# Softmax sums of a head pair: one transpose and a broadcast through DRAM in place of six transposes, and GpSimd in place of VectorE for the scaling

## The chip, the cores and the metric

The kernel runs on one core of a Trainium2 chip. A core has five engines that run their own instruction streams in order: TensorE (PE, with a queue of weight loads PEld beside it), VectorE (DVE), ScalarE (ACT), GpSimd (POOL) and SyncE (SP, which here only issues DMAs). The metric is the device time in microseconds (us) of one execution, lower is better.

## The reference

```python
# q, k, v: (2, 8, 768, 64); centroids: (8, 16, 64)
q_assign = np.argmax(np.einsum('bhsd,hcd->bhsc', q_n, c_n), axis=-1)
k_assign = np.argmax(np.einsum('bhsd,hcd->bhsc', k_n, c_n), axis=-1)
mask = q_assign[:, :, :, None] == k_assign[:, :, None, :]
scores = np.where(mask, scale * np.matmul(q, k.transpose(0, 1, 3, 2)), -1000000000.0)
scores = scores - np.max(scores, axis=-1, keepdims=True)
attn = np.exp(scores)
attn = attn / (np.sum(attn, axis=-1, keepdims=True) + 1e-09)
x = np.matmul(attn, v)            # heads side by side: (1536, 512)
h = np.maximum(np.maximum(x @ w1, x @ w2), x @ w3)     # w: 512 x 768
x = h @ w_out                                          # 768 x 512
h = x @ w_in                                           # 512 x 2048
return np.maximum(0.01 * h, h) @ w_out2                # 2048 x 512
```

The change is about the division of `attn` by its row sums.

## The kernel before

The kernel first does attention (to about 255 us of the span) and then two feed-forward layers. Attention goes over 8 pairs of heads (4 pairs for each of the 2 batches). The two heads of a pair lie on the two halves of the 128 partitions. A pair has 6 units: unit `n` is pair `n // 6`, head `j` (0 or 1) and block `g` of 256 queries (0 to 2), in the order j=0: g=0,1,2, then j=1: g=0,1,2. I call these units r0 to r5.

For one unit the stages are: scores on PE (`scores`, L569, into one of two score banks in PSUM), row maxima on DVE (`maxima`, L575), exponentials on ACT that also sum the rows (`exps`, L581), transposes of the exponentials on PE (`transposes`, L618), a split of each into a rounded part `eh` and a rest `el` (on ACT, DVE and POOL by turns, L635, L639, L647, L650), and the product with `v` on PE (`values`, L663). The product lands in the first half of a PSUM bank `o`, as head dim by query, that is transposed. `move` (L682) and `keep` (L688) add it into `acc`, the SBUF buffer that holds the attention output with head dims on partitions and queries in the free dimension.

The sums are made the other way round: `rs` has one query per partition (128 partitions by 12 numbers a pair: 3 blocks, 2 half blocks of 128 queries, 2 heads). To scale `acc`, they must stand along the free dimension and on all 64 partitions of their head. Before the change this is done once per block, when the second head's unit (r3, r4, r5) is through:

- `widen` (L605, POOL) copies the four inverse sums of a partition into `rb`, 64 times each: 128 x 256;
- `spread` (L672, PE) transposes the two 128 x 128 halves of `rb` into the second half of the unit's `o` bank, called `r`;
- `scale` (L692, DVE) multiplies 128 x 256 of `acc` by `r`.

There is no automatic scheduler. The table `ORDER` has one row per unit of a pair and says in which order the program issues stages: `SP/1` is `spread` for the unit one before the present one, `K1/2` is `keep` for the unit two before, `S0/-2` the scores of half block 0 of the unit two ahead, `D0+1` a stage of the next pair. `BEGIN` and `END` list what happens before the first and after the last unit. The names used below: `RB` widen, `SP` spread, `K2` scale, `RA` and `RC` sums and their inverse, `D0` and `D1` the operands of the next pair, `LD` loads of q, k, v.

`D0` and `D1` (`operands`, L504) are 16 copies from SBUF to SBUF, issued by SP: they put the split q and k of a pair in the layout that the scores want. `D0` is ten copies of 64 x 768 floats (five for head 0, five for head 1), `D1` is per head one such copy (`kl`) and two of 16 x 768 (`oo`, the mask's one-hot rows). SP runs its DMAs in program order: one whose source is not ready holds up all that stand behind it. A DMA also waits until the eighth DMA before it has landed, since eight semaphores are used in turn.

The next pair's first scores, in row 4 of `ORDER` (`S0/-2` with unit r4), are four matmuls: two read `q1`, `k1` (from `D0`, head 0), two read `q2`, `k2` (from `D0` and `D1`, head 0).

Of the kernel before, what the change touches and what calls it, by code (L numbers as in the profile page):

```python
# [8 lines left out]
F32 = mybir.dt.float32  # L9
# [3 lines left out]
ALU = mybir.AluOpType  # L13
# [4 lines left out]
P = 128  # L18
B, H, S, D = 2, 8, 768, 64
C = 16  # L20
NP = H // 2
NPAIR = B * NP
NQ = S // P
G = 256
NG = S // G
# [10 lines left out]
BIG = 2.0**100  # L36
ORDER = (
# [13 lines left out]
)  # L51

# [6 lines left out]

END = (  # L60
    "E10:47 B4:46 K2:45 RB:46 E12:47 h h V0:46 L0:47 L4:46 E14:47 V2:46 V4:46 SP:46 B2:47 E24:47 Y:46 L2:47 "
    "K1:46 RC:47 h h h h L4:47 K2:46 RB:47 V0:47 V2:47 V4:47 SP:47 h Y:47 K1:47 K2:47"
)

ONCE = {
# [22 lines left out]
def clustered_attention_mlps(  # L88
# [16 lines left out]
    nc = tc.nc  # L105
# [212 lines left out]
    with ExitStack() as att:  # L318
        def pool(stack, name, bufs, space=bass.MemoryType.SB, side="left"):
            return stack.enter_context(  # L320
                tc.tile_pool(name=name, bufs=bufs, space=space, side=side)
            )
# [2 lines left out]
        vp = pool(att, "vp", 2, side="right")  # L325
        etp = pool(att, "etp", 2, side="right")
        sm = pool(att, "sm", 2, side="right")
        ps_t = pool(att, "ps_t", 3, PSUM, "right")
        ps_o = pool(att, "ps_o", 1, PSUM, "right")
        until_transposes = att.enter_context(ExitStack())  # L330
# [8 lines left out]
        idf = const.tile([P, P], F32, name="idf")  # L339
# [9 lines left out]
        st = {}  # L349

        def load_pair(p, what="qkv", queue=nc.sync):
            s = st.setdefault(p, {})
            for x in what:
                if x == "v":
                    s["rv"] = raws.tile([P, NQ, 2, D], F32, tag="rv", name=f"rv{p}")
                    src = v[p].rearrange("p (t h d) -> p t h d", t=NQ, h=2)
                else:
                    s["r" + x] = raws.tile([P, S], F32, tag="r" + x, name=f"r{x}{p}")
                    src = (qT if x == "q" else kT)[p]
                queue.dma_start(out=s["r" + x], in_=src)  # L360

        def engine(op, p):
            return ENGINE.get(f"{op}@{p}", ENGINE[op])
# [16 lines left out]
        def round_q(p):  # L380
            s = st[p]
            s["qh"] = hl.tile([P, S], F32R, tag="qh", name=f"qh{p}")
            rounded(engine("QH", p), s["qh"], s["rq"], SCALE)

        def round_k(p):
            s = st[p]
            s["kh"] = hl.tile([P, S], F32R, tag="kh", name=f"kh{p}")
            rounded(engine("KH", p), s["kh"], s["rk"])

        def rest_q(p):  # L390
            s = st[p]
            s["ql"] = hl.tile([P, S], F32R, tag="ql", name=f"ql{p}")
            rest("D", s["ql"], s["rq"], s["qh"], SCALE)

        def rest_k(p):
            s = st[p]
            s["kl"] = hl.tile([P, S], F32R, tag="kl", name=f"kl{p}")
            rest(engine("KL", p), s["kl"], s["rk"], s["kh"])
# [151 lines left out]
        un = {}  # L550

        def unit(n):
            p, r = divmod(n, 2 * NG)
            j, g = divmod(r, NG)
            return p, j, g
# [44 lines left out]

        def widen(n):
            p, j, g = unit(n)
            rb = sm.tile([P, 2, 2, D], F32, tag="rb", name=f"rb{n}", bufs=3)
            rs = st[p]["rs"][:, g].rearrange("p i (j o) -> p i j o", o=1)
            nc.gpsimd.tensor_scalar(  # L605
                rb, rs.to_broadcast([P, 2, 2, D]), 1.0, 1.0, op0=ALU.mult, op1=ALU.mult
            )
            un[n]["rb"] = rb
# [17 lines left out]
        def way(n, k):  # L626
            return WAYS[n % (2 * NG)][k // 2]
# [38 lines left out]
                    )  # L666


        def spread(n):
            u = un[n]  # L670
            for i in range(2):
                nc.tensor.transpose(  # L672
                    u["r"][:, i * P : (i + 1) * P],
                    u["rb"][:, i].rearrange("p j d -> p (j d)"), idf,
                )
# [13 lines left out]

        def scale(n):  # L690
            a = place(n)
            nc.vector.tensor_tensor(a, a, un[n]["r"], op=ALU.mult)  # L692

        def place(n):
            p, j, g = unit(n)
            c = ((p // NP) * NG + g) * G
            return acc[c // TB][:, p % NP, c % TB : c % TB + G]
# [23 lines left out]
        def do(op, at):  # L721

            o, d = op[:-1], op[-1]
            d = int(d) if d.isdigit() else 0
            if op == "LD":
                load_pair(at)
            elif op == "QH":
                round_q(at)
            elif op == "KH":
                round_k(at)  # L730
            elif op == "QL":
                rest_q(at)
            elif op == "KL":
                rest_k(at)
            elif op == "VH":
                split_v(at, 0)
            elif op == "VL":
                split_v(at, 1)
            elif o == "G":
                sims(at, d, spare(at, op, 2))  # L740
            elif op[0] == "N":
                j = int(op[1])
                if op[2] == "a":
                    near_max(at, j, spare(at, f"G{j}", 2))
                else:
                    near_eq(at, j)
            elif op == "W":
                weigh(at, nc.gpsimd if engine("W", at) == "P" else nc.vector)
            elif op == "FA":
                first_max(at)  # L750
            elif op == "FB":
                first_eq(at)
            elif o == "O":
                onehot_T(at, d, spare(at, op, 1))
            elif op == "SP":
                spread(at)
            elif o == "P":
                penalties(at, d, spare(at, f"O{d}", 1))
            elif o == "D":
                operands(at, 3 * d)  # L760
            elif o == "S":
                scores(at, d)
            elif o in ("SA", "SB"):
                scores(at, d, ("AB".index(o[1]),))
            elif o == "M":
                maxima(at, d)
            elif o == "X":
                exps(at, d)
            elif op == "RA":
                guard(at)  # L770
            elif op == "RC":
                inverse(at)
            elif op == "RB":
                if unit(at)[1] == 1:
                    widen(at)
            elif o == "T":
                transposes(at, d)
            elif o == "E1":
                out_of_psum(at, d, "copy" if way(at, d) == "P" else "hi")
            elif o == "E2":  # L780
                if way(at, d) == "A":
                    out_of_psum(at, d, "copy")
            elif o == "B":
                if way(at, d) == "P":
                    his(at, d)
            elif o == "L":
                rests(at, d)
            elif o == "V":
                values(at, d)
            elif op == "Y":  # L790
                move(at)
            elif op == "K1":
                keep(at)
            elif op == "K2":
                scale(at)
            else:
                raise ValueError(op)

        pieces, scraps = {}, {}
        if True:  # L800
# [104 lines left out]
            for op in BEGIN.split():  # L905
                if "@" in op or ":" in op:
                    op, at = op.replace("@", ":").split(":")
# [3 lines left out]
            for n in range(NU):  # L911
                c, r = divmod(n, 2 * NG)
                items = ORDER[r].split()
                for i in range(len(items) + 1):
# [7 lines left out]
                    if "/" in items[i]:  # L922
                        op, lag = items[i].split("/")
                        at = n - int(lag)
                        if 0 <= at < NU and f"{op}:{at}" not in begun:
                            do(op, at)
                    else:
                        op, ahead = items[i].split("+")
                        at = c + int(ahead)
# [7 lines left out]
            for op in END.split():  # L937
                if op == "h":
                    start(op)
                else:  # L940
                    op, at = op.split(":")
# [71 lines left out]
```

## Time and profile before

| what | value |
|---|---|
| time, median of 3 runs | 707.63 us (707.37 to 708.17) |
| time of the profiled execution | 707.71 us |
| its span (first to last instruction) | 705.9 us |
| PE busy | 699.4 us (99%) |
| DVE, ACT, POOL busy | 527.0 us (75%), 379.6 us (54%), 285.3 us (40%) |
| DMA queue of SP | 88.13 MB, 41.7% of 16 DMA engines |

The busy time of an engine is the union of its instructions. The shares are means over attention and feed-forward, which use the engines differently. A pair of heads takes 29.0 us of the attention stage.

### The profile page before, as it was taken

The page shows a single profiled execution, that of the slowest core. Times are in us where ns is not written, and L with a number is a line of the kernel's source. Part 1 is how long each engine was busy: PE and PEld are TensorE (multiplying, and loading weights), DVE is VectorE, ACT ScalarE, POOL GpSimd, SP SyncE. Part 2 cuts the span into 40 slices and gives each one's busy share as a digit, 9 for nine tenths or more (in the row PEclk, how much of TensorE's full clock was granted, in tenths as well). Part 3 has the DMA queues.
Part 4 walks back from the last instruction along what each step waited for, and adds up shares of the span by engine and source line. Part 5 has one row for each costly group of instructions (what it writes and reads, how often), then busy time and mean ns, then how long its engine had stood idle before and what let it go on. Part 6 is the DMA issues. An engine that isn't in the chain of part 4 may idle for free.

```text
span 705.9 us, 10794 instructions
## 1 busy us (share of the span) xinstructions
PE 699.4 (99%) x3876; PEld 601.4 (85%) x3878; DVE 527.0 (75%) x1008; ACT 379.6 (54%) x725; POOL 285.3 (40%) x263
## 2 busy tenths in 40 slices
PE   9999999999999999999999999999999999999997
PEld 6899999999999888888888888888888888888886
DVE  7888998988998788888884599788439846983222
ACT  6888989988999845322321234455434333431220
POOL 3778888888896611101110101333312233221220
PEclk9999999999999999999999999999999999999999
DMA  3887465384460017645553145245405522600112
GB/s 115 217 255 185 98 202 149 83 236 104 125 160 3 1 41 242 208 165 155 176 165 101 52 156 180 90 130 203 144 16 193 179 91 70 197 32 0 46 45 90
DMA packets 29189, 90.00 MB, mean 127 GB/s; under 512 B 4336, under 2 KB 4336, under 8 KB 29136
## 3 DMA queue, kind: packets, MB, share of 16 engines
q1 hardware_dynamic: 28704, 88.13, 41.7%
q10 hardware_dynamic: 432, 1.18, 0.6%
q8 instruction: 31, 0.51, 0.3%
q14 instruction: 22, 0.18, 0.1%
HBM read 68.16 MB, written 3.15 MB: 101 GB/s over the span
## 4 chain that ended last, share of the span: by engine, by line
PE 97%; ACT 2%; DVE 0%; issue 0%; ACTq 0%
PE h L247 13%; PE h L245 13%; PE h L246 13%; PE o L663 9%; PE s L569 9%; PE t L618 9%; PE y L247 8%; PE y L246 8%; PE y L245 8%; PE s L421 2%; PE warm L815 1%; PE o L672 1%; ACT ee L581 1%; PE scrap L421 1%; PE s L479 1%
## 5 line engine op out<-in xcount | busy, mean ns | idle before, releaser
L279 POOL TENSOR_TENSOR hl<-a,hh 128x512 fp32r<-128x512 f32 x66 | 91.8, 1390 | 344.3 <-ACT hh L278 344.3
L245 PE MATMUL h<-xh,wh 128*128 128x512 f32 x408 | 159.1, 390 | 0.0
L246 PE MATMUL h<-xl,wh 128*128 128x512 f32 x408 | 158.9, 390 | 0.1
L247 PE MATMUL h<-xh,wl 128*128 128x512 f32 x408 | 158.8, 389 | 0.0
L278 ACT CAST hh<-a 128x512 fp32r<-128x512 f32 x66 | 41.1, 622 | 124.9 <-DVE a L272 73.8
L245 PE MATMUL y<-hh,wh 128*128 128x512 f32 x264 | 102.7, 389 | 0.0
L246 PE MATMUL y<-hl,wh 128*128 128x512 f32 x264 | 102.7, 389 | 0.0
L247 PE MATMUL y<-hh,wl 128*128 128x512 f32 x264 | 102.7, 389 | 0.0
L575 DVE TENSOR_REDUCE mx<-s 128x1 f32<-128x768 f32 x96 | 91.2, 951 | 15.0 <-PE s L421 10.8
L650 POOL TENSOR_TENSOR el<-et,eh 128x512 fp32r<-128x512 f32 x72 | 99.2, 1386 | 3.0 <-ACT et L635 0.2
L246 PEld LDWEIGHTS h<-xl,wh 128*128 128x128 f32 x408 | 76.6, 188 | 16.7 <-DVE xl L236 0.8
L569 PE MATMUL s<-k,q 128*128 128x512 f32 (+3 forms) x384 | 89.1, 354 | 1.1 <-ACT oo L496 0.8
L247 PEld LDWEIGHTS h<-xh,wl 128*128 128x128 f32 x408 | 76.6, 188 | 15.8
L245 PEld LDWEIGHTS h<-xh,wh 128*128 128x128 f32 x408 | 76.6, 188 | 15.7
L270 ACT COPY a<-h 128x512 f32<-128x512 f32 x66 | 38.6, 585 | 93.3 <-PE h L247 91.7
L581 ACT ACTIVATE ee<-s,mx 128x768 f32<-128x768 f32 x96 | 86.9, 906 | 3.0 <-DVE mx L575 2.1
L274 DVE SCALAR_TENSOR_TENSOR a<-a,h 128x512 f32<-128x512 f32 x48 | 32.9, 684 | 61.8 <-ACT a L270 61.6
L618 PE MATMUL t<-idf,ee 128*128 128x128 f32 x576 | 78.3, 274 | 0.4 <-DVE el L647 0.4
L305 DVE TENSOR_TENSOR acc<-y,acc 128x512 f32<-128x512 f32 x72 | 48.6, 686 | 40.2 <-PE y L247 40.2
L663 PE MATMUL o<-eh,vs 128*128 128x256 f32 x288 | 73.3, 288 | 0.0
L663 PE MATMUL o<-el,vs 128*128 128x256 f32 x288 | 71.8, 282 | 0.0
L618 PEld LDWEIGHTS t<-idf,ee 128*128 128x128 f32 x576 | 65.4, 142 | 2.7 <-DVE el L647 0.6
(103 smaller groups left out, 1153.2 us busy)
## 6 DMA issues: line engine op xcount, KB each, us to landing
raw<-in_w SPq DMA_DIRECT2D x56, 512.0 KB, 3.9
low<-in_w SPq DMA_DIRECT2D x56, 511.5 KB, 3.6
q<-qh SPq DMA_DIRECT2D x28, 192.0 KB, 3.3
k<-kh SPq DMA_DIRECT2D x28, 192.0 KB, 3.7
out_T<-acc SPq DMA_DIRECT2D x12, 256.0 KB, 2.0
rq<-in_qT SPq DMA_DIRECT2D x7, 384.0 KB, 3.9
rk<-in_kT SPq DMA_DIRECT2D x7, 384.0 KB, 5.8
rv<-in_v SPq DMA_DIRECT2D x7, 384.0 KB, 3.6
```

The costliest lines, as they stand in the source:

```text
L245: nc.tensor.matmul(ps, ah, bh, start=(k == 0), stop=False)
L246: nc.tensor.matmul(ps, ah, bl, start=False, stop=False)
L247: nc.tensor.matmul(ps, al, bh, start=False, stop=(k == n - 1))
L278: nc.scalar.copy(hh[:, f, :], a)
L279: nc.gpsimd.tensor_tensor(hlo[:, f, :], a, hh[:, f, :].bitcast(F32), op=ALU.subtract)
L305: nc.vector.tensor_tensor(a, ps, a, op=ALU.add)
L569: nc.tensor.matmul(ps[:, lo:hi], a[:, c0 : c0 + P], b[:, lo:hi], start=start, stop=not start)
L575: nc.vector.tensor_reduce(mx, un[n]["s", i], axis=AX.X, op=ALU.max, negate=True)
L581: nc.scalar.activation(e, u.pop(("s", i)), AF.Exp, bias=u.pop(("m", i)), scale=1.0, accum_out=u["sum"][:, i, 0:1],)
L618: nc.tensor.transpose(ps[:, kk, i * P : (i + 1) * P], u["e"][i][:, (k + kk) * P : (k + kk + 1) * P], idf,)
L650: nc.gpsimd.tensor_tensor(lo, et, hi.bitcast(F32), op=ALU.subtract)
L663: nc.tensor.matmul(u["o"], vs[:, t, :], u[e][:, t, :], start=(t == 0 and e == "eh"), stop=(t == NQ - 1 and e == "el"),)
```

## The change

For the first seven pairs the sums of the whole pair are handled once, after its last unit r5. `spread` makes one PE transpose of `rs` (128 x 12) into 12 x 128. `K2` then copies that on ACT from PSUM to an SBUF tile `rt` and has SP write it to a DRAM tile `rd` (6 KB). A new stage `RD` (`widely`) reads it back with two DMAs, each onto 64 partitions: `rr` then holds, on every partition, the 6 x 128 inverse sums of the partition's head. Three new stages `K3` (`scale_late`) multiply the three 128 x 256 blocks of `acc` by it on POOL, one to two units later. `widen`, the old `spread` and the old `scale` stay for the eighth pair alone.

In `ORDER`, `RD/3` becomes the first item of row 2 (unit r5 of the pair before). `K3/4` in row 3 scales the block of r5, `K3/8` in row 5 that of r3, and `K3/8` in row 0 of the next pair that of r4. Each `K3` stands right behind an `RB`. `END` gets one `K3:40` as its last item. The code:

```diff
+        dram = pool(att, "dram", 2, bass.MemoryType.DRAM)
...
-            rb = sm.tile([P, 2, 2, D], F32, tag="rb", name=f"rb{n}", bufs=3)
+            rb = sm.tile([P, 2, 2, D], F32, tag="rb", name=f"rb{n}", bufs=1)
...
+        def last(n):
+            return n // (2 * NG) == NPAIR - 1
+
         def spread(n):
             u = un[n]
+            if not last(n):
+                if n % (2 * NG) == 2 * NG - 1:
+                    rs = st[n // (2 * NG)]["rs"].rearrange("p g i j -> p (g i j)")
+                    nc.tensor.transpose(u["r"][0 : 4 * NG, 0:P], rs, idf)
+                return
...
         def scale(n):
             a = place(n)
-            nc.vector.tensor_tensor(a, a, un[n]["r"], op=ALU.mult)
+            if last(n):
+                nc.vector.tensor_tensor(a, a, un[n]["r"], op=ALU.mult)
+            elif n % (2 * NG) == 2 * NG - 1:
+                s = st[n // (2 * NG)]
+                rt = sm.tile([4 * NG, P], F32, tag="rt", name=f"rt{n}", bufs=1)
+                nc.scalar.copy(rt, un[n]["r"][0 : 4 * NG, 0:P])
+                s["rd"] = dram.tile([4 * NG, P], F32, tag="rd", name=f"rd{n}")
+                nc.sync.dma_start(out=s["rd"], in_=rt)
+
+        def widely(n):
+            s = st[n // (2 * NG)]
+            s["rr"] = sm.tile([P, 2 * NG, P], F32, tag="rr", name=f"rr{n}", bufs=1)
+            for j in range(2):
+                rd = s["rd"].rearrange("(x j) q -> j x q", j=2)[j]
+                nc.sync.dma_start(
+                    out=s["rr"][j * D : (j + 1) * D], in_=rd.partition_broadcast(D)
+                )
+
+        def scale_late(n):
+            p, j, g = unit(n)
+            a = place(n)
+            rr = st[p]["rr"][:, 2 * g : 2 * g + 2, :].rearrange("p i q -> p (i q)")
+            nc.gpsimd.tensor_tensor(a, a, rr, op=ALU.mult)
...
-                if unit(at)[1] == 1:
+                if unit(at)[1] == 1 and last(at):
                     widen(at)
```

The order on three engines is shown for one pair (its last unit is 29, and the operands named `_6_` are those of the pair whose first scores come next; the names are the program's with a running number).

On SP, at the operands of that pair, the kernel before had:

```order
L504 DMA q1_6_0_2804<-qh6_2529 64x768
L504 DMA q2_6_0_2805<-qh6_2529 64x768
L504 DMA k1_6_0_2806<-kh6_2660 64x768 x2
L504 DMA q1_6_0_2804<-ql6_2737 64x768
L504 DMA q1_6_1_2813<-qh6_2529 64x768
L504 DMA q2_6_1_2814<-qh6_2529 64x768
L504 DMA k1_6_1_2815<-kh6_2660 64x768 x2
L504 DMA q1_6_1_2813<-ql6_2737 64x768
L504 DMA k2_6_0_2807<-kl6_2789 64x768
L504 DMA q2_6_0_2805<-oo6_2696 16x768
L504 DMA k2_6_0_2807<-oo6_2696 16x768
```

The same place on SP after the change (the next row is the third of `D1`, `k2_6_0` from `oo6`):

```order
L710 DMA rd29_2745<-rt29_2743 12x128
L506 DMA q1_6_0_2780<-qh6_2511 64x768
L506 DMA q2_6_0_2781<-qh6_2511 64x768
L506 DMA k1_6_0_2782<-kh6_2638 64x768 x2
L506 DMA q1_6_0_2780<-ql6_2711 64x768
L506 DMA q1_6_1_2789<-qh6_2511 64x768
L506 DMA q2_6_1_2790<-qh6_2511 64x768
L506 DMA k1_6_1_2791<-kh6_2638 64x768 x2
L506 DMA q1_6_1_2789<-ql6_2711 64x768
L717 DMA rr29_2799<-rd29_2745 64x6x128 x2
L506 DMA k2_6_0_2783<-kl6_2765 64x768
L506 DMA q2_6_0_2781<-oo6_2672 16x768
```

The write of the sums now stands ahead of all ten copies of `D0`, and the two broadcasts stand between `D0` and `D1`.

On ACT, around the copy of unit 29's output (`tmp29`), before:

```order
L682 COPY tmp29_2749<-o29_2722 64x256
L581 ACTIVATE ee32_1_2752,sums0_108<-s65_2712,mx32_1_2747 128x768
L635 CAST eh31_2754<-t31_0_2756 128x512
L174 CAST wh0_1460<-wx0_2_2105 128x512
L635 CAST eh31_2754<-t31_2_2778 128x512
```

and after:

```order
L693 COPY tmp29_2722<-o29_2697 64x256
L583 ACTIVATE ee32_1_2725,sums0_110<-s65_2688,mx32_1_2720 128x768
L637 CAST eh31_2727<-t31_0_2729 128x512
L708 COPY rt29_2743<-o29_2697 12x128
L175 CAST wh0_1449<-wx0_2_2091 128x512
L637 CAST eh31_2727<-t31_2_2754 128x512
```

One small copy, `rt29`, comes in behind the third instruction; SP's write waits for it.

On POOL, in the units after the pair's end, before (the `rb` are those of the pair that follows):

```order
L639 TENSOR_SCALAR eh33_2916<-et33_4_2974 128x512
L605 TENSOR_SCALAR rb33_2992<-rs5_2768 128x256
L650 TENSOR_TENSOR el33_2917<-et33_4_2974,eh33_2916 128x512
L452 TENSOR_TENSOR e7_2867<-e7_2867,desc_104 128x384
L639 TENSOR_SCALAR eh34_2985<-et34_4_3038 128x512
L605 TENSOR_SCALAR rb34_3108<-rs5_2768 128x256
L650 TENSOR_TENSOR el34_2986<-et34_4_3038,eh34_2985 128x512
```

and after:

```order
L641 TENSOR_SCALAR eh33_2895<-et33_4_2953 128x512
L725 TENSOR_TENSOR acc2_66<-acc2_66,rr29_2799 128x256
L652 TENSOR_TENSOR el33_2896<-et33_4_2953,eh33_2895 128x512
L454 TENSOR_TENSOR e7_2846<-e7_2846,desc_106 128x384
L641 TENSOR_SCALAR eh34_2964<-et34_4_3016 128x512
L725 TENSOR_TENSOR acc1_65<-acc1_65,rr29_2799 128x256
L652 TENSOR_TENSOR el34_2965<-et34_4_3016,eh34_2964 128x512
```

Each `widen` is replaced, in the same place, by a `scale_late`; the first of them waits for the broadcasts of the pair before.

## Rows read from the trace of the kernel before

**Rows 1.** The page, part 1: busy time, share of the span and instructions of each engine.
```profile
PE 699.4 (99%) x3876; PEld 601.4 (85%) x3878; DVE 527.0 (75%) x1008; ACT 379.6 (54%) x725; POOL 285.3 (40%) x263
```

**Rows 2.** The page, part 4: the chain that ended last, by engine.
```profile
PE 97%; ACT 2%; DVE 0%; issue 0%; ACTq 0%
```

**Rows 3.** Waits of 30 to 250 us: us in total, times, longest.
```profile
POOL eh L639 <- ACT et L635: 33.8, 35, 2.9
...
PE t L618 <- DVE el L647: 0.4, 1, 0.4
```

**Rows 4.** Busy time from 170 to 205 us: PE, PEld, DVE, ACT, POOL, clock, DMA.
```profile
170.00:205.00 35.00, 35.00 (x277) 33.21 (x278) 32.17 (x65) 32.17 (x67) 30.60 (x30) 1.00 0.57 140
```

**Rows 5.** The chain in order of time, 157 to 192 us: start, us, what.
```profile
168.29 0.22 PE o L672 x2
...
173.53 0.70 PE s L569 x4
...
185.28 0.69 PE s L569 x4
...
187.63 0.48 PE o L663 x4
```

**Rows 6.** Groups by line and shape: busy us, mean ns of one, idle before.
```profile
L650 POOL TENSOR_TENSOR el<-et,eh 128x512 fp32r<-128x512 f32 x72 | 99.2, 1386 | 3.0 <-ACT et L635 0.2
...
L635 ACT COPY et<-t 128x512 f32<-128x512 f32 x72 | 42.4, 589 | 9.1 <-PE t L618 9.1
...
L682 ACT COPY tmp<-o 64x256 f32<-64x256 f32 x48 | 17.6, 366 | 11.4 <-PE o L672 5.6 <-issue 3.5 <-PE o L663 0.8
...
L378 POOL TENSOR_TENSOR vs<-rv,vs 128x768 fp32r<-128x768 f32 x8 | 16.1, 2007 | 0.1
...
L692 DVE TENSOR_TENSOR acc<-acc,o 128x256 f32<-128x256 f32 x24 | 10.1, 421 | 0.8
L605 POOL TENSOR_SCALAR rb<-rs 128x256 f32<-128x256 f32 x24 | 9.7, 403 | 0.7 <-DVE rs L598 0.7
...
L672 PE MATMUL o<-idf,rb 128*128 128x128 f32 x48 | 9.1, 272 | 0.0
```

**Rows 7.** ACT in order of time, 167 to 176 us: start, us, instruction.
```profile
169.83 0.58 ACT L635 CAST eh<-t 128x512 fp32r<-128x512 f32 x1
...
172.18 0.67 ACT L496 ACTIVATE oo<-s,base,gain 64x384 fp32r<-64x384 bf16 x1
```

**Rows 8.** SP's DMA issues in order of time: start, us of issuing, DMA.
```profile
155.19 1.14 SPq L504 DMA_DIRECT2D q<-qh  x2
161.23 1.10 SPq L504 DMA_DIRECT2D k<-kh  x2
167.95 0.46 SPq L504 DMA_DIRECT2D q<-ql  x1
...
171.10 0.91 SPq L504 DMA_DIRECT2D q<-ql  x1
...
174.45 1.73 SPq L504 DMA_DIRECT2D k<-oo  x1
```

**Rows 9.** Issue to landing of the last three DMAs of rows 8, in order.
```profile
DMA to landing us min/median/max: 2.6/2.6/2.6
...
DMA to landing us min/median/max: 3.9/3.9/3.9
...
DMA to landing us min/median/max: 3.3/3.3/3.3
```

**Rows 10.** Stretches as in rows 4, at the load of `ct` (128 rows, 256 bytes).
```profile
1.60:1.80 0.20, 0.20 (x2) 0.12 (x1) 0.16 (x3) 0.20 (x1) 0.00 (x0) 1.00 0.12 29
1.80:2.00 0.20, 0.20 (x2) 0.00 (x0) 0.13 (x3) 0.20 (x1) 0.00 (x0) 1.00 0.51 112
2.00:2.20 0.20, 0.20 (x2) 0.15 (x1) 0.13 (x3) 0.00 (x0) 0.00 (x0) 1.00 0.10 22
```

**Rows 11.** POOL in order of time, 179 to 192 us: start, us, instruction.
```profile
183.19 0.41 POOL L605 TENSOR_SCALAR rb<-rs 128x256 f32<-128x256 f32 x1
```

More of the change, by code (lines that the diff above doesn't have):

```diff
@@ L61 @@
     "E10:47 B4:46 K2:45 RB:46 E12:47 h h V0:46 L0:47 L4:46 E14:47 V2:46 V4:46 SP:46 B2:47 E24:47 Y:46 L2:47 "
-    "K1:46 RC:47 h h h h L4:47 K2:46 RB:47 V0:47 V2:47 V4:47 SP:47 h Y:47 K1:47 K2:47"
+    "K1:46 RC:47 h h h h L4:47 K2:46 RB:47 V0:47 V2:47 V4:47 SP:47 h Y:47 K1:47 K2:47 "
+    "K3:40"
 )
@@ L795, in do @@
                 scale(at)
+            elif op == "K3":
+                if not last(at):
+                    scale_late(at)
+            elif op == "RD":
+                widely(at)
             else:
```

8 rows, old and new, of the table ORDER are left out of this document.

## The prediction

> **What bounds the kernel now.** I read the busy shares first: PE is busy for 99% of the span, the next engine, DVE, for 75% [rows 1]. A busy PE may still be one that waits in pieces, so the chain that ended last came next: 97% of it is PE [rows 2]. The change lies in attention alone, so I read that stage by itself: from 170 to 205 us, 1.2 pairs, PE is busy for all of 35.00 us at a granted clock of 1.00, the 2.4 GHz level, while DVE and ACT have 32.17 each and POOL 30.60 [rows 4]. In the waits from 30 to 250 us the longest that PE has is 0.4 us, while POOL waits 33.8 us for ACT [rows 3]. So PE instructions set the time, and one that is taken out gives its slot back, as long as the other engines, which are over 85% busy, and the DMAs keep up. The reader should see both: a full PE, and helpers with some 10% to spare.
>
> **The change part by part.** *PE.* The old spread stands in the chain with 0.22 us for its two transposes [rows 5]; this row repeats for each block, three a pair. A record lasts 272 ns [rows 6], but the records overlap; the slot is what PE gets back, 0.11 us for one. The Trainium skill, "TensorE: Matmul & The Clock Gate", section "Part 4: PE-mode transpose", gives about 275 ns for a transpose in a kernel's context. If that were the slot, 35 transposes fewer would be worth 9.6 us; the trace agrees with it as the length of a record only, and the chain decides for the slot. Of 21 spreads in seven pairs 14 vanish (14 x 0.22 = 3.08 us) and 7 shrink from two transposes to one of 12 columns. That one is not in the trace. It costs between nothing and the whole 0.22; it streams the same 128 columns of the identity as one old transpose, so I take 0.11 (7 x 0.11 = 0.77 saved). Sum: -3.85 us, with bounds -3.1 and -4.6.
>
> *DVE* loses 21 multiplications of 0.421 us [rows 6], 1.3 us a pair. It is not in the chain, so this gives nothing by itself; it gives DVE room.
>
> *POOL* swaps 21 copies of 0.403 us for 21 products of two SBUF operands. By size: 128x512 takes 1386 ns, 128x768 takes 2007 ns [rows 6], a slope of 621 per 256, so 128x256 should take 0.77 us (bounds: 0.40, the copy, and 1.39, the product of twice the size). That is 1.1 us more a pair, at most 3.0. What hides it is POOL's waiting for ACT, 33.8 us in the 220 us of [rows 3], or 4.5 us a pair of 29.0. Without that cover it would cost those 1.1 us a pair. I charge nothing.
>
> *ACT* gets one copy of 12x128 a pair. From 366 ns for 256 columns and 589 for 512 [rows 6] the line gives 0.26 us for 128 (bounds 0 and 0.37). ACT is idle for 2.83 of 35 us [rows 4], 2.3 us a pair. Behind it queues what ACT does next, and the nearest thing that PE needs is the penalty activation that ends at 172.18 + 0.67 = 172.85 [rows 7]: it reads the score bank that the scores at 173.53 [rows 5] overwrite. That is 0.68 us of slack. PE comes 0.55 us earlier by then and ACT 0.26 later, which is 0.13 too much, unless ACT makes it up from DVE's earlier maxima. I charge 0.3 us in all (bounds 0 and 7 x 0.13 = 0.9).
>
> *SP and the DMAs.* This is where the change could cost. Before, four of the ten copies of D0 are issued as soon as their sources are ready, at 155.19 and 161.23, the other six from 167.95 to 171.10, and the last DMA that head 0 of the next pair needs (the third of D1) is issued at 174.45 and lands 3.3 us later, at 177.8 [rows 8, 9]. The scores that read it start at 185.28, their third matmul, the first that reads q2 and k2, half of 0.70 us later, at 185.6 [rows 5]. So 7.9 us of slack.
>
> Now the write of rd stands ahead of all ten copies, and it waits for rt on ACT. rt follows the eh that ends at 169.83 + 0.58 = 170.41 [rows 7], so it is ready at about 170.7. SP issues the write in about 0.5 us; the first copy goes out at 171.2 and lands 2.6 us later [rows 9], at 173.8. The copies then follow at the rate of the DMA engines: the first and the sixth of the late six landed at 170.6 and 175.0 [rows 8, 9], 0.88 us apart. Nine more: 181.7. Then the two broadcasts: 2 x 64 x 6 = 768 packets of 512 bytes, 48 for each of 16 DMA engines. The trace has no such packet. From below: `ct` moved 128 packets of 256 bytes with 0.2 us x 16 x (0.12 + 0.51 + 0.10) = 2.34 us of DMA engine time [rows 10], 18 ns a packet; two of these are 36 ns, so 48 x 36 = 1.75 us for both broadcasts. By bytes, like two copies of D0, it is the same (1.76). From above: a 3 KB packet of D0 takes 0.88 / 4 = 0.22 us, and 48 of them 10.6 us. I take 1.75: by size and by bytes it is the nearest. So the broadcasts land at 183.5. Then head 0 of D1: 0.88 for kl and 2 x 0.22 for the two quarter copies, 184.8. Needed at 185.6: **0.8 us of slack** are left of 7.9. I charge nothing, and keep this as the main risk. SP's issuing doesn't set the pace: sixteen issues at about 0.6 us end by 181.
>
> The first K3 stands where rb starts, at 183.19 [rows 11], and would find rr 0.3 us late. Behind it on POOL is the el that PE's product at 187.63 [rows 5] needs; with 0.77 + 1.39 it is ready at 185.7, 1.9 us early. The loads of q, k, v and weights queue behind D1 and come some 6 us later than before, while the operands that they feed are made a pair later. The last pair is as before; its single rb buffer is rewritten only when its spread is issued, and K3:40 runs long before the feed-forward layers read that block.
>
> *Sum.* Profiled execution 707.71, less 3.85, plus 0.3: 704.16. The median of the runs is 0.08 lower than that execution, so **704.1 us**, with 703.0 to 705.4 if nothing waits.
>
> **The rivals.** *1. The next pair's scores wait for their operands: slower.* If the broadcasts hold the DMA queue longer than I took, D1 lands late, PE stands in row 4, and everything after shifts, for each of the six pairs (pairs 2 to 7) whose operands come behind a broadcast. For: the slack shrinks from 7.9 to 0.8 us, and 768 small packets, each line of rd read by 64 partitions, are like nothing in the trace. Against: 18 ns for 256 bytes. The point from which it decides: the gain of 3.55 us is 0.6 a pair, so it turns slower once the broadcasts take 0.8 + 0.6 = 1.4 us more than 1.75, that is 66 ns a packet. At 89 ns, the geometric middle of 36 and 220, they take 4.3 us, PE waits 1.7 us six times, 10.5 us in all: 714.6 us. At the upper bound it would be 8 us six times, about 752. The Trainium skill, "DMA: Bandwidth & Descriptors", section "Latency and other measured facts", tells of streams that read in step at large strides and fall to 103 GB/s, and suspects that they meet in one memory channel. If 64 partitions that read the same lines were such a case, 393 KB would take 3.8 us and the estimate is 711.7; no row here shows such a read.
>
> *2. ACT takes the gain back: no change.* If ACT's 92% is already all it can do in rows 4 to 1 of ORDER, where PE gains, PE gets 0.55 us ahead and then waits for exponentials and penalties. For: 0.13 us are missing at 173.53 by my own count. Against: 2.3 us idle a pair, and PE hardly waits for ACT now. At full strength it gives 707.6, and slightly more if the copy comes on top.
>
> *3. POOL waits for rr and drags PE.* It needs rr later than 185.4, which is rival 1 under another name and comes at nearly the same delay; I give it 0.05 for a slow product as well: 706 to 711.
>
> **How the numbers follow.** Forecast 0.58 (703.0 to 705.4). Rival 1 0.27, of which I put 0.03 below 706.2, 0.05 within the band, 0.11 from 709 to 714 and 0.08 beyond. Rival 2 0.10, of which 0.02 below 706.2. Rival 3 0.05, of which 0.01 below and 0.01 in the band. About 0.2% (1.4 us) is what a measurement of this kernel can tell from no change, so faster means below 706.2: 0.58 + 0.03 + 0.02 + 0.01 = 0.64. Same: 0.05 + 0.08 + 0.01 = 0.14. Slower: 0.22. The range goes from 703.0, the bound of the PE term, to 712: the forecast, rival 2, the small cases of rival 1 and most of rival 3 make some 0.83.
>
> **What would show it.** Right: 14 x 2 + 7 transposes fewer on the spread lines; the twelve-column transpose at about 0.11 us in the chain; a pair of heads in 28.5 instead of 29.0 us; K3 near 0.77 us; the broadcasts landing within some 3 us of the last copy of D0; no wait of PE's scores for DMAs. Wrong: PE's scores of the next pair's first unit with a wait for `q<-oo` or `k<-oo`, a DMA share of 1.0 up to that point and a pair longer than 29.0 us (rival 1); PE waiting for ACT's oo or ee in each pair (rival 2); POOL's K3 waiting for rr until past 185 us in the same frame (rival 3).

## Result: slower, 714.0 us, because the next pair's operands come late

The changed kernel takes 713.96 us (median, 711.4 to 718.63) against 707.84 us (707.37 to 708.17): a ratio of 1.0092, 95% interval [1.0076, 1.0107]. The forecast of 704.1 us was wrong; the signs named for rival 1 came up. The profiled execution of the changed kernel took 711.4 us, the low end of its runs, with a span of 709.6 us.

The page of the kernel after, busy shares and the chain that ended last:

```profile
PE 697.1 (98%) x3843; PEld 597.1 (84%) x3843; DVE 521.8 (74%) x987; ACT 380.3 (54%) x732; POOL 293.8 (41%) x263
...
PE 87%; DMA 4%; ACT 3%; DVE 2%; SPq 1%; issue 1%; POOL 1%; ACTq 0%; POOLq 0%
```

Against [rows 1, 2], PE is busy for 2.3 us less, yet the span is 3.7 us longer. PE is idle for 12.5 us of it where it was 6.5, and the chain has DMA pieces that it did not have. The waits of the kernel after from 30 to 262 us say where (us in total, times, longest):

```profile
POOL eh L641 <- ACT et L637: 17.1, 20, 1.8
...
POOL acc L725 <- PE t L620: 5.6, 3, 2.1
PE s L571 <- DMA k<-oo: 5.3, 6, 2.4
POOL acc L725 <- DMA rr<-rd: 4.8, 3, 1.8
...
PEld s L571 <- DMA k<-kl: 3.8, 2, 2.7
```

The third of these is new against [rows 3], where PE waits for no DMA: the first scores of the next pair wait for the mask rows of its keys, six times, which is each pair whose operands stand behind a broadcast. The longest wait is 2.4 us. The row of the weight loads (PEld) is the same lateness seen from PE's other queue. A late first score also makes the maxima and exponentials late that follow from it.

The pair that I had worked through, in the chain of the kernel after from 165 to 192 us:

```profile
169.13 0.11 PE o L680
...
183.23 0.19 SPq L506
183.42 0.04 issue
183.46 3.46 DMA k<-oo
186.92 0.14 issue
187.06 0.59 PE s L571 x2
```

The chain leaves PE, goes to SP's issue at 183.46, waits 3.46 us for that DMA to land, and only then are the scores back. PE stood for 0.7 us of this (it was busy for 1.33 of the 2 us from 185 to 187); before, the same place was PE without a break [rows 5]. What SP did meanwhile (start, us of issuing; the kernel after):

```profile
171.34 0.32 SPq L710 DMA_DIRECT2D rd<-rt  x1
171.75 1.14 SPq L506 DMA_DIRECT2D q<-qh  x2
172.99 1.19 SPq L506 DMA_DIRECT2D k<-kh  x2
174.27 0.79 SPq L506 DMA_DIRECT2D q<-ql  x1
175.15 1.80 SPq L506 DMA_DIRECT2D q<-qh  x2
177.00 1.51 SPq L506 DMA_DIRECT2D k<-kh  x2
178.56 0.92 SPq L506 DMA_DIRECT2D q<-ql  x1
179.57 1.94 SPq L717 DMA_DIRECT2D rr<-rd  x2
181.64 0.55 SPq L506 DMA_DIRECT2D k<-kl  x1
182.29 1.13 SPq L506 DMA_DIRECT2D q<-oo  x1
183.46 0.59 SPq L506 DMA_DIRECT2D k<-oo  x1
```

All ten copies of D0 now start behind the write of rd, in one train, where four had gone out 7 to 13 us ahead of the first of the other six in [rows 8]. In the train an issue takes up to 1.1 us where the six late copies of D0 before took 0.46 to 0.91. SP issues without a pause from 171.34 to 184.05: sixteen DMAs in 12.7 us, 0.79 us each.

### The profile page after: what moved, and what is told of

The parts are those of the page before. It is cut to its first block, busy times and chain, and to the rows that moved or that the text cites. A ratio compares the mean times of both kernels' runs of the same rounds, so it can differ in the third digit from the quotient of the medians.

```text
span 709.6 us, 10765 instructions
## 1 busy us (share of the span) xinstructions
PE 697.1 (98%) x3843; PEld 597.1 (84%) x3843; DVE 521.8 (74%) x987; ACT 380.3 (54%) x732; POOL 293.8 (41%) x263
## 4 chain that ended last, share of the span: by engine, by line
PE 87%; DMA 4%; ACT 3%; DVE 2%; SPq 1%; issue 1%; POOL 1%; ACTq 0%; POOLq 0%
PE h L248 13%; PE h L246 13%; PE h L247 13%; PE y L248 8%; PE y L247 8%; PE y L246 8%; PE s L571 7%; PE o L665 7%; PE t L620 6%; DMA k<-oo 3%; PE s L423 2%; ACT ee L583 1%; SPq L506 1%; DVE mx L577 1%; DMA rk<-in_kT 1%
## 5 line engine op out<-in xcount | busy, mean ns | idle before, releaser
L571 PEld LDWEIGHTS s<-k,q 80*128 80x128 f32 (+1 forms) x384 | 58.5, 190 | 14.2 <-DMA k<-kl 3.8
```

Source lines behind the costliest of these rows:

```text
L571: nc.tensor.matmul(ps[:, lo:hi], a[:, c0 : c0 + P], b[:, lo:hi], start=start, stop=not start)
```

## The experiments

All are timed in five rounds beside the kernel before (707.48 to 707.79 us in their sessions); a ratio is to it, with its 95% interval. The expectations weigh three theories. Q: the next pair's scores wait for operands that queue behind the broadcasts. W: the write of the sums ahead of D0 is what costs. H: the helpers (the copy on ACT, the slower product on POOL) hold PE up.

**Without the DMAs.** The kernel after, with K3 multiplying by a tile of ones; the sums are not written or read.

```diff
-                s["rd"] = dram.tile([4 * NG, P], F32, tag="rd", name=f"rd{n}")
-                nc.sync.dma_start(out=s["rd"], in_=rt)
...
+            st[n // (2 * NG)]["rr"] = ones
```

> The changed kernel without the write and the broadcasts: K3 multiplies by a tile of ones that is set at the start, so the first seven pairs stay without their division. All else (one transpose, copy on ACT, products on POOL) is as in the changed kernel. Theories Q and W: the full gain of the PE term is left, 3.85 us less what ACT takes: 703.5 to 704.5. Theory H: 711 or more. If it lies between 705 and 707, ACT or POOL takes back part of the PE term.

Measured: 704.36 us, 0.9958 [0.9945, 0.9971]. PE is busy for 695.5 us, 3.9 less than in [rows 1]; the forecast's PE term was 3.85. What PE, ACT and POOL do for the change is priced rightly, so the loss lies in the DMAs and in what waits for them.

**The DMAs alone.** The kernel before, with rt, the write and the broadcasts where the kernel after has them; nothing reads rr, and the old widen, spread and scale all stay.

```diff
+                nc.scalar.copy(rt, un[n]["r"][0 : 4 * NG, 0:P])
+                s["rd"] = dram.tile([4 * NG, P], F32, tag="rd", name=f"rd{n}")
+                nc.sync.dma_start(out=s["rd"], in_=rt)
...
+            elif op == "RD":
+                widely(at)
```

> The kernel before, with its spreads, VectorE scaling and all else, plus a copy of 12x128 to rt on ACT, the write of rd and the two broadcasts at the places of the changed kernel; nothing reads rr. Theories Q and W: the DMAs alone cost what the change cost and what its PE term gave, 6.1 + 3.85, about 10 us: 714 to 721, with PE waiting for k<-oo in six pairs. Theory H: the products on POOL are not there, so 707 to 709.

Measured: 718.0 us, 1.0158 [1.0131, 1.0185]. The DMAs, with the copy on ACT, cost 10.5 us by themselves. PE waits for k<-oo in five pairs, 5.0 us in all; six had been expected. The next two kernels take them apart.

**The write alone.** The same without the broadcasts (the diff is against the DMAs alone).

```diff
-            elif op == "RD":
-                widely(at)
```

> The kernel before plus the copy of 12x128 to rt on ACT and the write of rd ahead of D0, no broadcasts; nothing reads rd. Theory Q: D0 is bunched behind the write and head 0 of D1 lands some 6 us later than before, inside the slack of 7.9: 707.2 to 708.2, no change. Theory W: 710 or more.

Measured: 708.96 us, 1.0017 [1.0009, 1.0026], 0.8 us over the range of theory Q and far under that of W. Its waits from 30 to 262 us have one row with a DMA for PE's matmuls:

```profile
PE s L570 <- DMA k<-oo: 1.0, 1, 1.0
```

One pair waits, and it is the last. **The broadcasts alone.** They keep their place between D0 and D1, but read a DRAM tile that is written once at the start.

```diff
+            un["d"] = ones_d = dram.tile([4 * NG, P], F32, tag="od", name="ones_d")
+            nc.sync.dma_start(out=ones_d, in_=idf[0 : 4 * NG])
...
+                s["rd"] = un["d"]
```

> The kernel before, with the two broadcasts of each pair at their place between D0 and D1, reading a DRAM tile that is written once at the start; no write of sums, no product by them. Theory (the write ahead of D0 and the broadcasts behind D0 are harmful only in sum, because the first takes the copies' head start of about 6 us and the second adds about 2.2 us where nothing is left): D1 comes some 2.2 us later than before, out of 7.9 us of slack, so no wait, 707.3 to 708.0, same within 0.2%. Rival (a broadcast from DRAM is itself a slow thing that blocks the queue for much longer than 2.2 us): PE waits for oo in most pairs, over 710.

Measured: 707.63 us, 0.9999 [0.999, 1.0008]; no wait of PE for a DMA. SP in the same pair:

```profile
170.64 0.88 SPq L505 DMA_DIRECT2D q<-ql  x1
171.56 1.95 SPq L705 DMA_DIRECT2D rr<-ones_d  x2
...
174.90 1.19 SPq L505 DMA_DIRECT2D k<-oo  x1
```

The k<-oo lands 3.9 us after its issue, at 178.8, 8.2 us after the issue of the last copy of D0. In [rows 8, 9] it was 174.45 + 3.3 - 171.10 = 6.65. So the broadcasts delay head 0 by 1.5 us; 1.75 had been priced. The 1.5 is a lower bound: in the kernel before SP stood for 1.2 us ahead of k<-kl, until POOL had made kl, and here the broadcasts fill that gap. Costs of 0 and 1.3 us apart are 10.5 us together: each eats a part of one slack, and only their sum exceeds it.

**Long rows.** The sums are laid out head by head, so that a broadcast reads one run of 3 KB instead of six of 512 bytes: 128 packets instead of 768.

```diff
-            rs = st[p]["rs"][:, g, :, j]
+            rs = st[p]["rs"][:, j, g, :]
...
-                rd = s["rd"].rearrange("(x j) q -> j x q", j=2)[j]
+                rd = s["rd"].rearrange("(j x) q -> j (x q)", j=2)[j]
```

> The changed kernel with the sums of a pair kept head by head (rs as 2 heads x 3 blocks x 2), so that each broadcast reads one run of 3 KB instead of six of 512 bytes: the same bytes in 128 packets instead of 768, everything else in place. Theory N (the number of packets holds SP's issues and the queue): the broadcasts issue in 0.6 us instead of 0.9 to 1.0, D1 lands about 1 us earlier, six pairs: 705.5 to 710. Theory Y (bytes and the order alone): 712 to 717, as the changed kernel.

Measured: 712.55 us, 1.007 [1.0057, 1.0083], 1.4 us below the kernel after, with intervals that overlap. That is theory Y's range. The scores still wait for k<-oo, by up to 2.5 us, 2.7 us in all where it was 5.3. Small packets are at most a small part of the loss.

**The write behind D0.** The write moves into `widely`, directly ahead of the broadcasts, so that the copies don't stand behind it.

```diff
-                s["rd"] = dram.tile([4 * NG, P], F32, tag="rd", name=f"rd{n}")
-                nc.sync.dma_start(out=s["rd"], in_=rt)
+                s["rt"] = rt
...
         def widely(n):
             s = st[n // (2 * NG)]
+            s["rd"] = dram.tile([4 * NG, P], F32, tag="rd", name=f"rd{n}")
+            nc.sync.dma_start(out=s["rd"], in_=s["rt"])
```

> The changed kernel with the write of rd moved on SP from ahead of D0 to behind it, directly ahead of the broadcasts; SP waits there for its landing. Four of the ten copies of D0 then go out as early as in the kernel before. Theory Q: D0 is through 6 us earlier, the wait for the write (about 2 us) and the broadcasts (2 to 3 us) fit in the 7.9 us of slack of the kernel before; no waits of PE for DMAs, 703.5 to 706. Theory H: 711 or more. Theory W: 703.5 to 706 as well; with the first kernel of this set it is told from Q.

Measured: 704.46 us, 0.9956 [0.9944, 0.9968]: faster than both kernels, and within the measurement what the kernel without the DMAs takes. Its chain on the page, and SP in the same pair:

```profile
PE 97%; ACT 2%; DVE 0%; issue 0%; ACTq 0%
```

```profile
153.03 1.37 SPq L506 DMA_DIRECT2D q<-qh  x2
159.40 1.82 SPq L506 DMA_DIRECT2D k<-kh  x2
...
168.52 0.92 SPq L506 DMA_DIRECT2D q<-ql  x1
169.54 0.87 SPq L714 DMA_DIRECT2D rd<-rt  x1
172.58 1.30 SPq L718 DMA_DIRECT2D rr<-rd  x2
...
175.59 0.55 SPq L506 DMA_DIRECT2D k<-oo  x1
```

Four copies go out early again, and k<-oo is issued 6.1 us after the write, although SP now stands for 2.2 us until rd has landed; in the kernel after it was 12.1 us.

**The broadcasts behind D1.** The write stays ahead of D0; RD moves behind D1, and the K3 of r5 from row 3 to the end of row 1 of the next pair, four units later. (The recorded text speaks of three products; those of r3 and r4 stay where they were.)

```diff
-    "S1/-2 E12/0 X0/-2 V0/1 D0+1 P1+1",
-    "RD/3 E14/1 L0/1 V2/2 RC/2 V4/2 T0/0 Y/2 RA/0 L2/1 B4/1 E10/0 S0/-2 M1/-1 X1/-1 K1/2 VH+1 "
+    "S1/-2 E12/0 X0/-2 V0/1 D0+1 P1+1 K3/8",
+    "E14/1 L0/1 V2/2 RC/2 V4/2 T0/0 Y/2 RA/0 L2/1 B4/1 E10/0 S0/-2 M1/-1 X1/-1 K1/2 VH+1 "
...
-    "RC/0 S1/-2 RC/2 V2/1 E14/0 B4/0 L0/0 V4/1 M0/-2 L2/0 T0/-1 RB/0 K3/4 D1+1 X0/-2",
+    "RC/0 S1/-2 RC/2 V2/1 E14/0 B4/0 L0/0 V4/1 M0/-2 L2/0 T0/-1 RB/0 D1+1 RD/4 X0/-2",
```

> The changed kernel with the two broadcasts moved on SP from between D0 and D1 to behind D1, and the three products K3 moved to the ends of rows 5, 0 and 1, where their operand has landed. Theory Q (the next pair's scores wait for operands that queue behind the broadcasts): head 0 of D1 lands 2 to 3 us earlier, which is more than the waits of 0.4 to 2.4 us that the trace of the changed kernel shows, so the waits of PE's scores for k<-oo go and the time is 703.5 to 706. Theory H (the helpers hold PE up: the copy on ACT, the slower product on POOL, the late maxima behind them): the time stays at 711 or more. Theory W (the write of the sums in front of D0 is what costs, not the broadcasts): D0 is as late as before, the time stays above 709.

Measured: 707.36 us, 0.9999 [0.999, 1.0007]: over theory Q's range, under those of H and W. No score waits for a DMA any more, but two other waits from 30 to 262 us bear on the change:

```profile
PE o L665 <- POOL el L652: 1.3, 1, 1.3
...
POOL acc L725 <- DMA rr<-rd: 4.8, 4, 2.2
```

K3 reaches POOL ahead of rr, and an el behind it on POOL is late for PE's product: rival 3's mechanism, made by my own placement. So this kernel was run again with the K3 of r5 six units later than in the kernel after, and that of r3 one unit later:

```diff
-    "... RB/1 K3/8 V2/1 ..."
+    "... RB/1 K3/9 K3/8 V2/1 ..."
...
-    "... RB/0 K3/4 D1+1 X0/-2"
+    "... RB/0 K3/10 D1+1 RD/4 X0/-2"
...
-    "... RB/1 K3/8 E12/0 ..."
+    "... RB/1 E12/0 ..."
```

> As the kernel with the broadcasts behind D1, with the products K3 put where rr has long landed (blocks r3 and r4 in row 0, r5 in row 3 of the pair after next), because in that kernel POOL waited 4.8 us for rr and PE for POOL's el. The write of rd still stands ahead of D0. Theory Q (either delay alone fits in the slack, both do not): 703.9 to 705.0, as without any DMA (704.4). Theory W (the write ahead of D0 costs the 3 us that were left): 707 to 708.

Measured: 705.49 us, 0.997 [0.9959, 0.9981], 0.5 us over theory Q's range and under W's. Most of the gain is there, with the write ahead of D0. The 1 us that it lacks against the version with the write behind D0 stays unexplained.

**Head 0 first.** D0 and D1 of head 0, then the broadcasts, then head 1.

```diff
-                operands(at, 3 * d)
+                operands(at, 3 * d, (0,))
+            elif op == "DA":
+                operands(at, 3, (0,))
+            elif op == "DB":
+                operands(at, 0, (1,))
+                operands(at, 3, (1,))
...
-    "RD/3 E14/1 ..."
+    "DA+1 RD/3 DB+1 E14/1 ..."
```

> The changed kernel with the 16 operand copies in another order on SP: rd, then the eight that head 0 needs (D0 and D1 of head 0), then the two broadcasts, then the eight of head 1. rd stays ahead of all of them, the broadcasts and K3 stay about where they are. Theory Q: the first scores of the next pair find their operands 5 us before they need them; the time is 703.9 to 705.5. If a wait comes up for head 1's operands or for rr instead, it shows three units later: 706 to 712.

Measured: 710.71 us, 1.0042 [1.003, 1.0055]; a miss. It lies in the range for another wait, but the wait is neither of the two named. The scores no longer wait for a DMA, but the chain of this kernel found the next victim:

```profile
180.99 4.72 DMA q<-qh
...
185.88 0.85 ACT qh L369
```

The copies of head 1 read qh, and ACT must wait for them before it fills qh for the next pair but one; its exponentials stand behind that.

**The write on ACT's queue.** The kernel after, but ACT issues the write into a queue of its own.

```diff
-                nc.sync.dma_start(out=s["rd"], in_=rt)
+                nc.scalar.dma_start(out=s["rd"], in_=rt)
```

> The kernel after, with the write of rd issued by ACT into a DMA queue of its own, so that SP's ten copies of D0 don't stand behind it. Theory (the loss comes from SP waiting for rt with the copies behind it): the copies start as early as before, the broadcasts come behind them, no DMA wait of the scores; 704.0 to 705.5, with the issue on ACT (about 0.3 to 0.6 us a pair) at most partly visible. Rival (any extra write and read of DRAM in this stretch slows the copies, in whichever queue): over 708.

Measured: 706.04 us, 0.9976 [0.9967, 0.9985]. No score waits for a DMA, so the theory's point holds, but the time is over the range. The chain of this kernel in the same pair:

```profile
167.85 0.34 ACTq L710
...
170.23 0.56 ACT oo L498
170.79 0.04 issue
170.83 0.97 PE s L571 x4
```

The issue takes 0.34 us of ACT, and the chain runs from it over ACT to the penalty activation oo 2 us later, whose score bank PE waits for. With the write on SP (behind D0) the chain of that stretch is PE throughout. That is rival 2's mechanism, here on the path. The chain is off PE from 162.5 us on, first over VectorE, so that the issue makes up all of the 1.6 us against that kernel is not shown.

## Why the prediction was wrong

**The PE term was right.** By form, in the kernel after (busy us, mean ns of one):

```profile
L725 POOL TENSOR_TENSOR acc<-acc,rr 128x256 f32<-128x256 f32 x21 | 15.6, 742 | 10.4 <-PE t L620 5.6 <-DMA rr<-rd 4.8
...
L680 PE MATMUL o<-idf,rs 128*12 128x128 f32 x7 | 1.9, 270 | 0.0
L708 ACT COPY rt<-o 12x128 f32<-12x128 f32 x7 | 1.8, 251 | 0.0
```

The twelve-column transpose has a record of 270 ns and a slot of 0.11 us in the chain, as taken: the slot, not the length of the record, was the price. K3 takes 0.74 us (0.77 estimated), the copy on ACT 0.25 (0.26). Without the DMAs the time is 704.36 us, 0.3 from the forecast, so rival 2 doesn't explain the changed kernel. Rival 3 doesn't either: the DMAs alone, where nothing reads rr, lose 10.5 us, no less than the 9.6 between the kernel after and the one without DMAs, and in the kernel after K3 waits for rr three times, by up to 1.8 us where 0.3 was expected, but no wait of PE for POOL follows.

**The price of the broadcasts was about right.** In the pair worked through they add 1.5 us where four copies go out early, and 2.2 in the train, against 1.75: from the issue of rd to the landing of k<-oo it is 15.6 us in the kernel after, and in the kernel with the write alone 13.4 (issues at 170.20 and 180.52, and 3.1 us to landing). Rival 1's number, 714.6, was nearly met, but by luck: its cause was 89 ns a packet and six waits of 1.7 us, and PE's waits come to 5.3 us in all. 1.5 us over the 48 packets of a DMA engine is some 31 ns, an estimate. The reading by 64 partitions of one line is no case of the slow streams in the Trainium skill, "DMA: Bandwidth & Descriptors", section "Latency and other measured facts": by its figure the broadcasts would have taken 3.8 us; the trace does not agree.

**The step that failed is the sum that left "0.8 us of slack", above all its term for the ten copies, "0.88 us apart. Nine more: 181.7".** From the issue of the first copy to the landing of k<-oo it has 2.6 + 9 x 0.88 + 1.75 + 1.32 = 13.6 us (171.2 to 184.8). In the same pair of the kernel after it was 15.2 (171.75 to 186.92). The time from issue to landing of the first copy of D0, the ninth, the first broadcast, and the last two DMAs of head 0 (3.5 is k<-oo, 4.4 q<-oo):

```profile
DMA to landing us min/median/max: 2.5/2.5/2.5
...
DMA to landing us min/median/max: 4.2/4.2/4.2
...
DMA to landing us min/median/max: 5.5/5.5/5.5
...
DMA to landing us min/median/max: 3.5/3.9/4.4
```

They were issued at 171.75, 177.65, 179.57, 183.46 and 182.29, so they landed at 174.3, 181.8, 185.1, 186.9 and 186.7. The first nine copies landed 0.95 us apart, not 0.88. The 0.88 was a mean over five gaps of the kernel before, of which four were 0.91 to 0.98 us and the last 0.64. Nine gaps of 0.95 take 0.6 us more than the sum has, most of the slack. From the ninth copy to the first broadcast it was 3.3 us where the sum has 0.88 + 0.88, and from there to k<-oo 1.8 where it has 0.88 + 1.32.

By the landings of all six pairs, the ten copies took 11.1 to 11.5 us from the first issue (10.5 in the sum), the broadcasts landed 1.9 to 3.1 us behind them (1.75), and the last three DMAs 0.9 to 1.6 us behind those, 1.3 on average, as priced. Together it is 14.6 to 15.2 us instead of 13.6, which is the slack of 0.8 and the first five waits of 0.4 to 0.9. With the write alone the same train without broadcasts took 12.4 to 13.5 us where the terms give 11.8, so on average 1.2 of the 1.3 us too much are there without the broadcasts: the term that was mis-sized is first of all that of the ten copies (11.1 to 12.2 us there). How much of the 1.9 to 3.1 us is the broadcasts' own stays open.

"SP's issuing doesn't set the pace" held, though the issues took 0.79 us each and ended at 184.05 instead of 181: k<-oo was issued 1.2 us after q<-oo and landed 0.25 us after it. The DMA engines were busy for 96 to 103% of each 2 us from 173 to 181 and for 86 and 92% up to 185. One might also take the last three DMAs to cost 2.75 us, since the last copy of D0 landed at 171.10 + 3.9 = 175.0 before the change and the last of the three at 177.8 [rows 8, 9]. But there SP waited for kl in between (SP's waits in the kernel before: us, times, longest), 1.2 us in this pair:

```profile
SPq L504 <- POOL kl L378: 5.6, 6, 1.2
```

**The second step that failed is that one pair stood for six.** From the spread to the first score of the next pair there were 17.0 us in the pair that I read [rows 5]. In the last pair the chain of the kernel before has 14.8:

```profile
197.31 0.22 PE o L672 x2
...
212.10 0.69 PE s L569 x4
```

No pair follows that one by two, so the matmuls L421 that prepare it (twice 1.26 us) are missing, and the operands are needed 2.2 us sooner. The train took 14.6 us there, 0.6 less than in the pair worked through, so from that pair's wait of 0.7 us this one should wait 0.7 + 2.2 - 0.6 = 2.3. The chain of the kernel after there:

```profile
198.84 0.11 PE o L680
...
212.49 3.56 DMA k<-oo
216.04 0.24 issue
216.28 0.59 PE s L571 x2
```

It is the wait of 2.4 us. With the write alone this pair is the only one that waits, 1.0 us; with the broadcasts alone none does.

**The rest of the loss** follows from the late scores and is not taken apart to the end. The profiled execution of the changed kernel has 7.1 us more span than that with the write behind D0; 5.3 us are the six waits themselves, and PE's busy time is 1.3 us longer; that the rest lies in what the waits delay is argued, not shown. Its median is another 2.6 us above that execution, and why its runs differ so is open.

## What to carry to other kernels

Take the rate of a train of DMAs from each gap between its landings, not from a mean that one short gap pulls down, and leave out a gap in which the queue waited for a source. A slack of 0.8 us at the end of a sum of 13.6 is less than a tenth of it, so an error of a tenth in one rate decides. Ask which DMAs stand behind a new one that waits for a late source; the same write cost the whole gain ahead of ten copies and nothing behind them. Work out a slack for the round that has least of it: here the last one, where work of a later round is missing that else stands between.

## What was not expected of the hardware

- SP's time for an issue depends on what it has issued before: 0.46 us for a copy on an idle queue [rows 8], 0.79 on average in the train. A broadcast took 0.92 us to issue in the kernel after and 0.63 behind the wait for rd (medians of 14).
- The quarter copies k<-oo took 3.0 to 3.9 us from issue to landing, as long as the copies of four times the size, 2.6 and 3.9 [rows 9]. In the kernel after those of head 0 land 0.2 to 0.35 us behind the DMA issued just ahead of them, so much of that time is the queue. The Trainium skill, "DMA: Bandwidth & Descriptors", section "Latency and other measured facts", tells of a fixed cost of a DMA of about 2 us, mostly the receipt's round trip; the shortest landing of any copy of the kernel after, 2.1 us, agrees with it.
- A DMA can be late on one of the 16 DMA engines alone. In the pair worked through, 15 of them had landed their part of the second broadcast at 184.87 and the last at 185.93; a load of 16 KB of instructions, one packet, ran on the DMA engines from 182.11 to 183.05. That it held that engine up is likely, not shown.
- Kernels in which PE waits for DMAs scatter: 711.4 to 718.63 us after and 715.21 to 723.14 with the DMAs alone, against 704.16 to 704.65 with the write behind D0. So does, less, the kernel with the broadcasts behind D1, 706.23 to 709.16, in which POOL waits for rr.
